# Linear-attention numerators in three rounds of 11, 11 and 10 heads instead of four rounds of 8, a memory output with one reciprocal, and a new engine order

## The chip, the core and the metric

The kernel runs on one core of a Trainium2 chip. The metric is the device time of one execution in microseconds; "span" is the length of the profiled execution, 1.7 us shorter than its timed value.

Engines are named as in the profile: PE (matmuls), PEld (their weight loads), DVE (VectorE), ACT (ScalarE), POOL (GpSimd), SP (the queue that issues most DMAs). A ratio below is the mean time of one kernel's fast runs over the mean of the kernel before's fast runs in the same rounds on the same chip. It is therefore not quite the ratio of the medians quoted beside it.

## The reference, cut to what matters

Two attention mechanisms read the same input of 2048 rows and 640 columns, with 32 heads of 20 columns; a gate mixes them.

```python
# A: linear attention with features softmax(pq), softmax(-pq)
num = einsum('bhqf,bhfd->bhqd', phi_q, kv)
den = einsum('bhqf,bhf->bhq', phi_q, z)[..., None] + 1e-06
a = (num / den).reshape(B, S, D) @ wo
# B: per segment of 512 rows, softmax attention plus a memory of earlier segments
o = sigmoid(beta) * a_mem + (1 - sigmoid(beta)) * a_dot
b = o.reshape(B, S, D) @ wo_B
return g * a + (1 - g) * b          # g = sigmoid(sum(x * gate_w))
```

## The kernel before

Every piece of work is an "op": one function that emits one or a few instructions, with what it reads and writes. Ops are numbered as they are created. A table `ORDER` gives each engine the list of op numbers it runs, in that order; each engine then runs its list in that order and waits where data are missing. A schedule model inside the kernel only turns the table into a program. Copies out of PSUM ("evacuations") can stand in the list of ACT or of DVE (a copy of the output takes 431 ns on ACT and 490 on DVE); the table decides.

```python
ORDER = {
    "PE": "29*7 73*3 77*2 80 88 104 89 82 120 90*2 ...",   # 29*7: seven ops from 29 on
    "ACT": "0 76 79 28 86 101 109 99 ...", "DVE": "27 72 81 70 83 68 93 ...",
    "POOL": "...", "SP": "1*3 10 5 11 13 4 8 7 6 9 100 ...",
}   # ... cut
```

The kernel lays out PSUM as four working banks `w` and four more that hold the attention scores `st`. The numerators of A ("a3") take four rounds for each chunk of 128 rows. One round is one bank:

```python
PARTS = (((0, 0, 7), (1, 0, 2)), ((1, 2, 5), (2, 0, 4)), ((2, 4, 4), (3, 0, 5)),
         ((3, 5, 2), (4, 0, 7)))
for qt in (2 * hf, 2 * hf + 1):          # a quarter: 8 heads, two signs, 22 columns each
    # PE: four small matmuls w <- Eq, KVD
    # ACT or DVE: dz = copy of 16 denominators out of the bank
    # DVE: xx = w * dz swapped; rr = sum over signs; rr = 1/rr; cs = w * gate * rr
    # DVE: ts = w * cs, 320 elements; then the bank is free
# POOL, once per two quarters: oA = ts[:, 0] + ts[:, 1]
```

The output of B for one group of four heads, with `Cdm` holding the gate products:

```python
for x, bk in enumerate(bks):             # local result, memory result: one bank each
    rd[x] = reciprocal(w_denominator)    # DVE, 16 elements
rd = rd * Cdm                            # DVE; a POOL op is ordered behind it (lk=True)
tdm[x] = w * rd[x]                       # DVE, 320 elements each, frees the bank
# POOL: oB = tdm[0] + tdm[1]
```

The softmax here doesn't subtract the row's maximum and nothing guards it: scores larger than these inputs give would overflow.

## Time and profile before

| | before |
|---|---|
| time, median of the first 4 runs | 291.47 us |
| span of the profile | 289.5 us |
| the 80 score exponentials (128x2048, ACT): end of the 5th, 40th, 80th | 43.7, 151.6, 268.0 us |
| late stretch (40th to 80th exponential) | 116.3 us |

The score exponentials serve as clock marks. Every kernel runs 80 of them, spread from 25 to 268 us, so the time at which the 5th, 40th and 80th ends cuts the span into a start, an early stretch (projections, key side), a late stretch (numerators, output projection) and a tail. Their ends come from the timeline, start plus duration.

The page of the kernel before, its part 1 (busy time, share of the span, instructions):

```profile
PE 280.5 (97%) x3764; PEld 191.9 (66%) x3777; DVE 229.7 (79%) x850; ACT 246.9 (85%) x353; POOL 189.2 (65%) x333
```

Part 4 of the same page, the chain of waits by engine (a queue's own time is marked with a q):

```profile
PE 80%; DVE 14%; DMA 3%; issue 1%; ACT 0%; DVEq 0%
```

PE's 97% rests on modelled ends, as the profile's own legend says. The median start-to-start distance of two matmuls of 320 columns is 136 ns where the record says 299; for 300, 340 and 512 columns the distances are 127, 144 and 215 ns, the records 291, 308 and 379. So the records of neighbours overlap. The stretches by time, here 160 to 272 us (columns: length, then busy time and instructions of PE, PEld, DVE, ACT, POOL, then granted clock, DMA share and GB/s):

```profile
160.00:272.00 112.00, 109.54 (x1607) 74.49 (x1617) 104.41 (x500) 103.60 (x123) 78.75 (x115) 1.00 0.61 133
```

DVE and ACT are both busy over 92% of this stretch (104.4 and 103.6 of 112 us). The groups of instructions of a numerator round (line, engine, operation, tiles, shape, count | busy us, mean ns of one | idle before):

```profile
L1044 DVE TENSOR_TENSOR ts<-w,cs 128x320 f32<-128x320 f32 x64 | 30.6, 486 | 1.4
L1040 DVE SCALAR_TENSOR_TENSOR cs<-w,gS,rr 128x16 f32<-128x16 f32 x64 | 14.2, 230 | 0.6
L1038 DVE RECIPROCAL rr<-rr 128x8 f32<-128x8 f32 x64 | 12.2, 198 | 0.7
L1032 DVE TENSOR_TENSOR xx<-w,dz 128x16 f32<-128x16 f32 x64 | 10.2, 169 | 0.8
L712 DVE CAST osb<-w 128x320 bf16<-128x320 f32 x6 | 2.9, 490 | 5.2 <-PE w L1086 5.2
```

A product of 16 elements takes 169 ns and one of 320 takes 486. That is 1.04 ns per element, which leaves an estimate of 152 of the 169 ns as the fixed part of the small one. That is the ground of the change. The last line is an output evacuation on DVE.

### The profile page before, as it was taken

What the parts mean: (1) busy time and instruction counts of PE and PEld (TensorE: products, weight loads), DVE (VectorE), ACT (ScalarE), POOL (GpSimd) and SP (SyncE); (2) the same over time, 40 slices, a digit from 0 to 9 for tenths busy, and PEclk for the clock granted to TensorE, in tenths of its full rate; (3) what the DMA queues carried; (4) which work ended last, traced back from release to release, by engine and by line L of the source; (5) the groups of instructions that cost most, each with busy time, mean ns of one, the idle gap of its engine ahead of it and who ended that gap; (6) DMA issues with size and microseconds to landing.
All of it is one profiled execution on the core that took longest, in us unless ns stands there. A gap on an engine that the chain in (4) does not pass through costs nothing.

```text
span 289.5 us, 9800 instructions
## 1 busy us (share of the span) xinstructions
PE 280.5 (97%) x3764; PEld 191.9 (66%) x3777; DVE 229.7 (79%) x850; ACT 246.9 (85%) x353; POOL 189.2 (65%) x333
## 2 busy tenths in 40 slices
PE   7899999999999999999999999999999999999995
PEld 3666676676676667676766566567766657667873
DVE  0774577888789999689968999988998999999820
ACT  3366799998999999999899999998999999988222
POOL 7045369789965899778282858474866586688600
PEclk9999999999999999999999999999999999999999
DMA  7998796745915432615059484824695748565342
GB/s 210 300 230 148 133 242 75 139 115 99 126 39 137 128 104 73 104 55 133 2 129 296 92 186 125 163 82 111 168 174 115 138 106 199 125 100 131 105 106 64
DMA packets 87976, 38.42 MB, mean 133 GB/s; under 512 B 69882, under 2 KB 83834, under 8 KB 87930
## 3 DMA queue, kind: packets, MB, share of 16 engines
q1 hardware_dynamic: 87274, 37.39, 57.7%
q8 instruction: 29, 0.48, 0.7%
q10 hardware_dynamic: 656, 0.41, 0.5%
q14 instruction: 17, 0.14, 0.2%
HBM read 5.61 MB, written 15.60 MB: 73 GB/s over the span
## 4 chain that ended last, share of the span: by engine, by line
PE 80%; DVE 14%; DMA 3%; issue 1%; ACT 0%; DVEq 0%
PE w L745 36%; PE w L1086 14%; PE w L1166 9%; PE st L1138 7%; PE w L988 4%; DVE ts L1044 4%; PE w L1019 3%; PE w L888 2%; DVE cs L1040 2%; DVE rr L1038 1%; PE w L1231 1%; DMA WkB<-in_B_wk_dram 1%; DVE tdm L1214 1%; DMA x_nat<-in_A_x_dram 1%; PE w L1185 1%
## 5 line engine op out<-in xcount | busy, mean ns | idle before, releaser
L1144 ACT ACTIVATE PT<-st 128x2048 bf16<-128x2048 f32 x80 | 151.4, 1893 | 4.9 <-PE st L1138 3.8
L1150 POOL TENSOR_SCALAR_AFFINE_SELECT PT<-PT 128x512 bf16<-128x512 bf16 x128 | 79.4, 637 | 41.3 <-ACT PT L1144 12.6
L745 PEld LDWEIGHTS <-xT 128*128 128x128 bf16 x800 | 72.4, 97 | 34.0 <-issue 9.1
L867 POOL TENSOR_TENSOR EkN<-Ek,krec 128x640 bf16<-128x640 bf16 x32 | 40.5, 1275 | 4.3 <-DVE phik L778 1.2
L1166 PEld LDWEIGHTS <-PT 128*128 128x128 bf16 x1280 | 39.8, 96 | 5.3 <-issue 0.8
L1166 PE MATMUL w<-vB,PT 128*128 128x21 bf16 x1280 | 41.5, 172 | 0.1
L745 PE MATMUL w<-WqB,xT 128*128 128x320 bf16 x160 | 36.0, 299 | 0.3 <-ACT kq L710 0.2
L745 PE MATMUL w<-WvA,xT 128*128 128x340 bf16 (+1 forms) x160 | 35.2, 299 | 0.0
L745 PE MATMUL w<-WkB,xT 128*128 128x320 bf16 x160 | 34.5, 299 | 0.2 <-ACT xT L691 0.2
L1048 POOL TENSOR_TENSOR oA<-ts 128x320 bf16<-128x320 f32 x32 | 27.4, 864 | 10.8 <-DVE dz L712 3.0
L745 PE MATMUL w<-WkA,xT 128*128 128x320 bf16 x160 | 33.5, 299 | 0.0
L745 PE MATMUL w<-WvB,xT 128*128 128x321 bf16 (+1 forms) x160 | 33.3, 300 | 0.1
L1086 PE MATMUL w<-WoA,oTA 128*128 128x320 bf16 x160 | 32.3, 299 | 0.2
L1086 PE MATMUL w<-WoB,oTB 128*128 128x320 bf16 x160 | 32.3, 299 | 0.0
L1138 PE MATMUL st<-kqT 32*128 32x384 bf16 (+3 forms) x512 | 31.7, 300 | 0.5 <-ACT PT L1144 0.5
L1044 DVE TENSOR_TENSOR ts<-w,cs 128x320 f32<-128x320 f32 x64 | 30.6, 486 | 1.4
L988 PE MATMUL w<-xT,WqA 128*128 128x512 bf16 x87 | 26.7, 379 | 0.8 <-DVE ts L1044 0.2
L1019 PE MATMUL w<-KVD,Eq 128*128 128x88 bf16 (+3 forms) x256 | 26.8, 207 | 0.6
L859 DVE TENSOR_REDUCE ksum<-Ek 128x32 f32<-128x640 bf16 x32 | 25.2, 804 | 2.5 <-ACT Ek L852 2.4
L1220 POOL TENSOR_TENSOR oB<-tdm 128x320 bf16<-128x320 f32 x24 | 20.6, 863 | 7.6 <-DVE dz L712 2.7
L1019 PEld LDWEIGHTS <-Eq 128*128 128x128 bf16 x256 | 19.2, 97 | 9.2 <-issue 2.8
L852 ACT ACTIVATE Ek<-w 128x320 bf16<-128x320 f32 x64 | 24.2, 452 | 1.3 <-PE w L745 1.0
(113 smaller groups left out, 445.7 us busy)
## 6 DMA issues: line engine op xcount, KB each, us to landing
kd<-kq SPq DMA_DIRECT2D x32, 256.0 KB, 2.3
od<-oA SPq DMA_DIRECT2D x16, 160.0 KB, 1.9
out_dram<-osb SPq DMA_DIRECT2D x32, 80.0 KB, 1.8
od<-oB SPq DMA_DIRECT2D x12, 160.0 KB, 1.9
WqB<-in_B_wq_dram SPq DMA_DIRECT2D x2, 400.0 KB, 4.7
WvB<-in_B_wv_dram SPq DMA_DIRECT2D x2, 400.0 KB, 4.6
WvA<-in_A_wqkv_dram SPq DMA_DIRECT2D x1, 800.0 KB, 6.3
WoA<-in_A_wo_dram SPq DMA_DIRECT2D x1, 800.0 KB, 5.3
```

The costliest lines, as they stand in the source:

```text
L745: nc.tensor.matmul(w[:, 0:width], lhsT=T["xT"][:, c, sc * P:(sc + 1) * P], rhs=T[Wn][:, c, lo:lo + width], start=(c == 0), stop=(c == KC - 1))
L859: op("DVE", 0.74, lambda sgn=sgn: nc.vector.tensor_reduce(out=T["ksum"][js][:, H * sgn:H * sgn + H], in_=T["Ek"][ik][:, sgn].rearrange("p ...
L867: op("POOL", 1.22, lambda sgn=sgn: nc.gpsimd.tensor_tensor(out=T["EkN"][ie][:, 0:2 * D].rearrange("p (h x f) -> p h x f", x=2, f=DH)[:, :, ...
L988: nc.tensor.matmul(w, lhsT=T["WqA"][:, c, t * P:(t + 1) * P], rhs=T["xT"][:, c, s * L:(s + 1) * L], start=(c == 0), stop=(c == KC - 1))
L1019: nc.tensor.matmul(w[:, c0:c0 + m * E2], lhsT=T["Eq"][j][:, sgn, qc * P:(qc + 1) * P], rhs=T["KVD"][:, sgn, OFF[t] + a:OFF[t] + a + m, :]. ...
L1044: op("DVE", dve_t(320), lambda w, c3=c3, qt=qt: nc.vector.tensor_tensor(out=T["ts"][d][:, :, 8 * (qt % 2):8 * (qt % 2) + 8], in0=vw(w)[:, ...
L1048: op("POOL", 0.82, lambda: nc.gpsimd.tensor_tensor(out=T["oA"][o][:, 320 * hf:320 * hf + 320].rearrange("p (h d) -> p h d", d=DH), in0=T[" ...
L1086: nc.tensor.matmul(w[:, 0:320], lhsT=T[nm][j][:, k5, :], rhs=T[Wo][:, k5, hf * 320:hf * 320 + 320], start=(i == 0), stop=(i == 9))
L1138: nc.tensor.matmul(st4[:, i, o:o + w], lhsT=T["kqT"][j][r:r + 32, 0, c * P:(c + 1) * P], rhs=T["kqT"][j][r:r + 32, 1, c * P:L], start=True ...
L1144: op("ACT", act_t(2048), lambda: nc.scalar.activation(out=T["PT"][slot], in_=st4, func=ACT.Exp, scale=SCALE_B), r=("st4",), w=(("PT", slot ...
L1150: nc.gpsimd.affine_select(out=v, in_=v, pattern=[[0, 4], [1, P]], compare_op=ALU.is_ge, fill=0.0, base=0, channel_multiplier=-1)
L1166: nc.tensor.matmul(w[:, j * 84 + i * V1:j * 84 + (i + 1) * V1], lhsT=T["PT"][slot][:, i, o + (j - c) * P:o + (j - c + 1) * P], rhs=T["vB"] ...
```

## The change

Its intent is to pay the fixed part less often. Eleven heads with two signs and 22 columns are 484 columns and still fit a working bank, which the kernel lays out as 512 fp32 columns, so three rounds do what four did. The memory output multiplies first and takes one reciprocal for both banks instead of two; the gate coefficients are stored inverted for it. All engine orders are new. The tile `ts` now has three buffers of one round each instead of two of a pair of rounds. The diff, cut to its core:

```diff
 ORDER = {                                   # all five lists new; SP begins
-    "SP": "1*3 10 5 11 13 4 8 7 6 9 100 132 ...",
+    "SP": "1*4 10 5 8 13 11 7 6 9 116 148 ...",
 ...
-    PARTS = (((0, 0, 7), (1, 0, 2)), ((1, 2, 5), (2, 0, 4)), ((2, 4, 4), (3, 0, 5)),
-             ((3, 5, 2), (4, 0, 7)))
+    PARTS = (((0, 0, 7), (1, 0, 5)), ((1, 5, 2), (2, 0, 8), (3, 0, 3)), ((3, 3, 4), (4, 0, 7)))
+    NHG = 11
 ...
-        for qt in (2 * hf, 2 * hf + 1):
+        for q in (2,) if hf else (0, 1):
 ...                                         # the six small ops now on 22 / 11 / 440 elements (third round: 20 / 10 / 400)
-        op("POOL", 0.82, ... oA[320 columns] = ts[:, 0] + ts[:, 1])   # once per two rounds
+            op("POOL", ..., ... oA[DH * nh columns] = ts[:, 0] + ts[:, 1])   # every round
 ...
         for x, bk in enumerate(bks):
-            rd[x] = reciprocal(w_denominator)
-        rd = rd * Cdm                        # lk=True
+            rd[x] = w_denominator * Cdm[x]
+        rd = reciprocal(rd)
 ...                                         # gates(), beta(): one more reciprocal each
```

## The prediction

> **What bounds the kernel now.** No single engine: three run nearly full. The page's first part shows PE 97%, ACT 85%, DVE 79%, POOL 65% of a 289.5 us span. PE's 97% is modelled ends. From start-to-start distances in the trace (N=320: 136 ns, N=21: 25 ns) the matmuls need about 263 us, so PE has some 16 us of holes after its first projection at 8.7 us. Busy time by stretch: between 60 and 160 us ACT is busy 95.5 of 100 us and DVE 83.8; between 160 and 272 us (the linear-attention numerators, "a3") DVE is 104.4 of 112, ACT 103.6. The chain of waits gives PE 80% and DVE 14%; its DVE pieces (ts, cs, rr, tdm) lie almost all in 160-272 us. From 272 us on it is PE alone: 80 output matmuls back to back in 11.0 us.
>
> **What the change does.**
> 1. a3 handles 11/11/10 heads per PSUM bank instead of four times 8: 48 rounds of six small operations instead of 64. The groups show 168+169+164+198+230+486 ns per round, but DVE overlaps neighbours: median start-to-start 119+117+119+120+150+408 = 1033 ns, 66 us in all. For 22/11/440 elements, at the trace's 1.04 ns per element (reciprocal about 6), I estimate 1200 ns, 58 us in all. DVE thus gains about 8.5 us of occupancy, all in 160-272 us. [...] a copy of 16 elements takes 168 ns, one of 320 takes 490.
> 2. PE: 256 numerator matmuls become 224 with the same columns: about 0.3 us.
> 3. POOL: 32 adds of 864 ns become 48 of about 570-620 ns (estimate): +1.5 us.
> 4. Memory-attention output: two reciprocals (239 ns) and one product (210) become two products (about 169) and one reciprocal of 32 (353, from the ksum reciprocal of that size): about zero. The product no longer orders a POOL instruction behind it (5.7 us of POOL waits), but POOL has slack.
> 5. New engine order. Counting the table: ACT keeps its load in sum (about -1 us), but takes about 4 us more evacuations before its tenth big exponential and 4 us fewer after its fortieth. Matmul work ahead of each score group is nearly unchanged; about 20 us remain after the last one in both.
>
> **On the critical path.** PE's work stays, so only its holes can shrink: some 16 us, perhaps 8 of them in 160-272 us. ACT, 92-95% busy, becomes the next limit there. The first 160 us and the PE-bound tail give nearly nothing. I expect about half of the late holes: 4 us.
>
> **Prediction.** 287.5 us, range 284.5 to 290.3 (8 in 10). Faster by over 2%: 0.2; within 2%: 0.77; slower by over 2%: 0.03.
>
> **What would show it.** DVE busy about 8 us (6-10) lower, nearly all in 160-272 us; ts at about 608 ns x48; DVE's share of the chain from 14% to under 9%, PE's up; ACT and POOL busy within 2 us; the last score exponential ending 3-5 us earlier than 268 us; the time from there to the end unchanged (about 21 us); 0 to 160 us within 1 us.
>
> **What would make it wrong.** The new order may close (or open) holes in the first 160 us too; DVE may have been the late phase's sole limit, then up to 8 us; or bigger rounds hold PSUM banks longer.

One clause of item 1 is cut where the mark stands, since it did not come from a run of this case; the two measured copies behind it, 168 and 490 ns, stay. Half of some 8 us of late holes is 4 us, and 291.5 less 4 is the 287.5 us forecast.

## The result, and the profile after

The changed kernel takes 289.76 us (median of 11 runs, 288.87 to 290.14) against 291.63 (16 runs): ratio 0.9932, 95% interval 0.9920 to 0.9944. That is 2.0 us, half of the 4.0 us forecast. It lies inside the range and within 2%, the likeliest of its three cases; the size of the gain is what was wrong. Part 1 of its page, busy time by engine:

```profile
PE 280.2 (97%) x3733; PEld 191.7 (67%) x3745; DVE 223.0 (78%) x766; ACT 247.7 (86%) x346; POOL 191.8 (67%) x349
```

Part 4 of its page, the chain of waits by engine:

```profile
PE 76%; DVE 17%; ACT 3%; issue 2%; DVEq 0%; ACTq 0%
```

Its stretch from 160 to 272 us, columns as before:

```profile
160.00:272.00 112.00, 109.59 (x1578) 73.93 (x1585) 100.68 (x414) 100.44 (x114) 81.73 (x130) 1.00 0.59 137
```

DVE has 84 instructions fewer over the whole span, but only 3.7 us less busy time in the window from 160 to 272 us, and its share of the chain rose. The groups that answer to those shown before:

```profile
L1046 DVE TENSOR_TENSOR ts<-w,cs 128x440 f32<-128x440 f32 x32 | 19.3, 612 | 1.4
L1046 DVE TENSOR_TENSOR ts<-w,cs 128x400 f32<-128x400 f32 x16 | 9.2, 573 | 0.8
L1042 DVE SCALAR_TENSOR_TENSOR cs<-w,gS,rr 128x22 f32<-128x22 f32 x32 | 7.4, 238 | 0.5
L1040 DVE RECIPROCAL rr<-rr 128x11 f32<-128x11 f32 x32 | 6.8, 218 | 0.5
L1034 DVE TENSOR_TENSOR xx<-w,dz 128x22 f32<-128x22 f32 x32 | 5.5, 176 | 0.3
L709 DVE CAST osb<-w 128x320 bf16<-128x320 f32 x11 | 5.2, 484 | 10.0 <-issue 5.0 <-PE w L1088 3.1 <-ACT osb L707 1.7
```

The duration of ts is what the prediction put it at (about 608 ns; 612 at 440 elements, and 573 at 400, which the prediction did not list apart). The durations also fit the 1.04 ns per element of the profile before: counted on from its 486 ns at 320 elements, it gives estimates of 569 and 611 ns for 400 and 440. The last line shows a leak: the new order puts 11 output evacuations on DVE instead of 6.

Where did 2 us come from? The marks of both kernels, from the timeline of ACT. Each fence has the 5th, the 40th and the last score exponential (columns: start us, duration us, engine, line, operation; a bracket gives the idle time before it and what ended it). Before:

```profile
41.69 1.98 ACT L1144 ACTIVATE PT<-st 128x2048 bf16<-128x2048 f32 x1
149.77 1.88 ACT L1144 ACTIVATE PT<-st 128x2048 bf16<-128x2048 f32 x1
266.10 1.88 ACT L1144 ACTIVATE PT<-st 128x2048 bf16<-128x2048 f32 x1
```

After:

```profile
40.17 1.98 ACT L1146 ACTIVATE PT<-st 128x2048 bf16<-128x2048 f32 x1
148.01 1.88 ACT L1146 ACTIVATE PT<-st 128x2048 bf16<-128x2048 f32 x1 [0.19 <-PE st L1140]
263.91 1.88 ACT L1146 ACTIVATE PT<-st 128x2048 bf16<-128x2048 f32 x1
```

The 5th ends 1.5 us earlier, at 42.2 us, some 116 us before the first numerator. The last ends 2.2 us earlier. So three quarters of the gain were made where no numerator runs. Part of that is chance: the start varies from profile to profile. Eight profiles with the old start (the kernel before and seven experiments below that leave it alone) put the 5th end at 43.7 to 44.6 us, mean 44.1. Three with the new start put it at 41.9 to 42.6, mean 42.2. The start is worth about 1.9 us. From the 5th end on, the stretches hardly vary between profiles (the early one is 108.0 or 108.1 us in all eight with the old start):

| stretch, us | before | after |
|---|---|---|
| start, to the end of the 5th exponential (means of 8 and of 3 profiles) | 44.1 | 42.2 |
| early, 5th to 40th | 108.0 | 107.7 |
| late, 40th to 80th | 116.3 | 115.9 |
| tail, from the 80th to the end | 21.5 | 21.7 |

The late stretch, for which the change was made, gave 0.4 us. (The rows add up to 2.4 us where the timed runs give 2.0; the rest lies within the spread of the start.)

### The profile page after: what moved, and what is told of

It reads as the page before. It is cut to its first block, busy times and chain, and to the rows that moved or that the text cites. A ratio compares the mean times of both kernels' runs of the same rounds, so it can differ in the third digit from the quotient of the medians.

```text
span 287.5 us, 9664 instructions
## 1 busy us (share of the span) xinstructions
PE 280.2 (97%) x3733; PEld 191.7 (67%) x3745; DVE 223.0 (78%) x766; ACT 247.7 (86%) x346; POOL 191.8 (67%) x349
## 4 chain that ended last, share of the span: by engine, by line
PE 76%; DVE 17%; ACT 3%; issue 2%; DVEq 0%; ACTq 0%
PE w L742 38%; PE w L1088 9%; PE w L1168 8%; PE st L1140 7%; DVE ts L1046 5%; PE w L987 3%; PE w L887 2%; ACT PT L1146 2%; PE w L1020 2%; DVE cs L1042 2%; DVE tdm L1215 1%; DVE rr L1040 1%; PE st L585 1%; PE w L1232 1%; DVE rr L1037 1%
## 5 line engine op out<-in xcount | busy, mean ns | idle before, releaser
L1168 PEld LDWEIGHTS <-PT 128*128 128x128 bf16 x1280 | 40.7, 96 | 5.9 <-issue 2.1
L1168 PE MATMUL w<-vB,PT 128*128 128x21 bf16 x1280 | 43.1, 172 | 0.0
L742 PE MATMUL w<-WvB,xT 128*128 128x320 bf16 (+1 forms) x160 | 37.0, 300 | 0.0
L742 PE MATMUL w<-WkB,xT 128*128 128x320 bf16 x160 | 36.6, 299 | 0.1
L1050 POOL TENSOR_TENSOR oA<-ts 128x220 bf16<-128x220 f32 (+1 forms) x48 | 30.3, 638 | 9.4 <-DVE ts L1046 4.8
L742 PE MATMUL w<-WvA,xT 128*128 128x340 bf16 (+1 forms) x160 | 33.4, 299 | 0.1
L1088 PE MATMUL w<-WoA,oTA 128*128 128x320 bf16 x160 | 31.4, 298 | 0.4 <-DVE ts L1046 0.2
L1046 DVE TENSOR_TENSOR ts<-w,cs 128x440 f32<-128x440 f32 (+1 forms) x48 | 28.4, 599 | 2.2
L1020 PE MATMUL w<-KVD,Eq 128*128 128x154 bf16 (+5 forms) x224 | 24.9, 213 | 0.3 <-DVE tdm L1215 0.2
L1215 DVE TENSOR_TENSOR tdm<-w,rd 128x320 f32<-128x320 f32 x48 | 21.6, 485 | 0.9
```

The costliest lines, as they stand in the source:

```text
L742: nc.tensor.matmul(w[:, 0:width], lhsT=T["xT"][:, c, sc * P:(sc + 1) * P], rhs=T[Wn][:, c, lo:lo + width], start=(c == 0), stop=(c == KC - 1))
L1020: nc.tensor.matmul(w[:, c0:c0 + m * E2], lhsT=T["Eq"][j][:, sgn, qc * P:(qc + 1) * P], rhs=T["KVD"][:, sgn, OFF[t] + a:OFF[t] + a + m, :]. ...
L1046: op("DVE", dve_t(2 * nh * DH), lambda w, nh=nh, vw=vw, tv=tv: nc.vector.tensor_tensor(out=tv("ts"), in0=vw(w)[:, :, :, 0:DH], in1=tv("cs" ...
L1050: op("POOL", 0.04 + 0.00244 * nh * DH, lambda h0=h0, nh=nh, tv=tv: nc.gpsimd.tensor_tensor(out=T["oA"][o][:, DH * h0:DH * (h0 + nh)].rearr ...
L1088: nc.tensor.matmul(w[:, 0:320], lhsT=T[nm][j][:, k5, :], rhs=T[Wo][:, k5, hf * 320:hf * 320 + 320], start=(i == 0), stop=(i == 9))
L1168: nc.tensor.matmul(w[:, j * 84 + i * V1:j * 84 + (i + 1) * V1], lhsT=T["PT"][slot][:, i, o + (j - c) * P:o + (j - c + 1) * P], rhs=T["vB"] ...
```

## The experiments

Theory A: the gain is the start, which the new order improved by the way, and the numerator rework gives about nothing. Rival B: the start differs by chance, and the rework gives the gain.

What differs at the start is visible in the timelines. Before, SP issues three of the four first input chunks and only four loads later the fourth; PE then waits for it, and DVE's list is headed by a small product that waits for another load. Kernel before (PE at line 681 transposes an input chunk; the bracket gives the idle time and what ended it):

```profile
0.81 1.34 SPq L537 DMA_DIRECT2D x_nat<-in_A_x_dram  x3
4.64 0.34 SPq L537 DMA_DIRECT2D x_nat<-in_A_x_dram  x1
7.21 0.30 DVE L667 TENSOR_TENSOR WphiD<-Wc,m 128x140 bf16<-128x140 bf16 x1 [6.00 <-DMA Wc<-in_A_w_phi_dram]
7.43 0.48 DVE L693 COPY xT<-w 128x640 bf16<-128x640 bf16 x1
8.22 0.45 PE L681 MATMUL w<-ident_b,x_nat 128*128 128x128 bf16 x5 [1.42 <-DMA x_nat<-in_A_x_dram]
```

Changed kernel, the same pieces: four loads in a row, DVE begins with a copy of transposed input, and PE's last transpose comes 1.8 us earlier.

```profile
0.81 1.82 SPq L534 DMA_DIRECT2D x_nat<-in_A_x_dram  x4
5.00 0.49 DVE L690 COPY xT<-w 128x640 bf16<-128x640 bf16 x1 [3.80 <-PE w L678]
6.43 0.44 PE L678 MATMUL w<-ident_b,x_nat 128*128 128x128 bf16 x5
```

### x3_early: one load earlier

```diff
-    "SP": "1*3 10 5 11 13 4 8 7 6 9 ...",
+    "SP": "1*4 10 5 11 13 8 7 6 9 ...",
```

> The kernel before, with one entry of the sync engine's order moved: the load of the fourth input chunk is issued straight behind the first three (it stood four loads later, issued at 4.64 us, and PE waited 1.42 us for it). Theory A (the whole gain of the change is this start, the numerator rework gives about nothing): ratio 0.993 to 0.996, the 1.7 us of PE holes that a DMA ends in the first 12 us gone, and every score exponential 1.3 to 1.8 us earlier. Theory B (the start differs by chance from run to run; the rework gives the gain): ratio 0.998 to 1.002.

Measured: 291.62 us against 291.50, ratio 1.0012 (0.9991 to 1.0032). No gain: this is the range that was set down for theory B. The profile shows why theory A need not fall with it. The load came early, but the phi weights' load behind it was issued at 3.54 us instead of 3.06, and DVE's list still began with the product that needs those and now started at 7.66 us instead of 7.21:

```profile
7.66 0.31 DVE L673 TENSOR_TENSOR WphiD<-Wc,m 128x140 bf16<-128x140 bf16 x1 [6.46 <-DMA Wc<-in_A_w_phi_dram]
7.88 0.49 DVE L699 COPY xT<-w 128x640 bf16<-128x640 bf16 x1
8.42 0.85 PE L751 MATMUL w<-WkB,xT 128*128 128x320 bf16 x5 [0.38 <-DVE xT L699]
```

The wait named in the profile had a second one right behind it (PE stands 0.38 us for DVE's copy). Theory A named one cause of the start too few.

### after_x3_late: the same load put back in the changed kernel

```diff
-    "SP": "1*4 10 5 8 13 11 7 6 9 ...",
+    "SP": "1*3 10 5 8 13 4 11 7 6 9 ...",
```

> The changed kernel with that one load put back to its old place in the queue. Theory A: ratio to before 0.997 to 1.002, the gain gone. Theory B: ratio 0.992 to 0.995 as the changed kernel itself.

Measured: 291.77 us, ratio 1.0027 (0.9998 to 1.0056). The whole gain is gone, as theory A said. The entry is thus needed for the gain of the given order, though x3_early shows that it does not bring the gain alone. In its profile the 5th exponential ends 2.6 us later than in the changed kernel's (44.8) and the span is 2.6 us longer; from the 5th end on both need 245.3 us. In this pair a shift of the start passes through to the end one to one.

### start_fix: both waits taken out of the kernel before

```diff
-    "SP": "1*3 10 5 11 13 4 8 7 6 9 ...",   "DVE": "27 72 81 70 83 68 93 ...",
+    "SP": "1*4 10 5 11 13 8 7 6 9 ...",     "DVE": "27 81 83 72 70 68 93 ...",
```

> The kernel before with the fourth input chunk's load issued right behind the first three, and with DVE's first six operations reordered so that the two copies of transposed input stand ahead of the three small products that wait for the phi weights' load (in x3_early DVE stood 6.5 us at their head). Numerators and the rest as before. Theory A (the changed kernel's gain is its start, and a shift of the start goes through to the end one to one, as after_x3_late showed: 2.6 us later at the fifth score exponential, 2.6 us later at the end): fifth exponential 1.0 to 1.6 us earlier, ratio 0.994 to 0.997. Theory B (the start is worth nothing without the new numerators): 0.998 to 1.002.

Measured: 290.85 us against 291.64, ratio 0.9964 (0.9952 to 0.9977): 1.0 us faster with the numerators untouched. The 5th exponential ends at 43.4 us, 0.7 under the mean of the old start (0.2 under the first profile; 1.0 to 1.6 were expected), and from there to the end it needs 245.8 us as before. PE's unbroken projections begin at 7.48 us there, at 8.51 before and at 6.71 in the changed kernel, so about half of the start's gain is accounted for. The rest of it lies in other entries of the new lists and is not taken apart.

### memout_only and after_old_memout: the memory output by itself

The first puts the new memory output, gates and beta into the kernel before; the second puts the old ones into the changed kernel. The op numbers do not change, so each keeps its kernel's order.

```diff
 # memout_only, in the kernel before
-            rd[x] = reciprocal(w_denominator)
-        rd = rd * Cdm
+            rd[x] = w_denominator * Cdm[x]
+        rd = reciprocal(rd)
```

> The kernel before with only the memory-output part of the change (product before reciprocal, coefficients inverted in gates and beta), old order, old numerators. Both theories: ratio 0.997 to 1.003; DVE busy within 1 us. A gain over 0.4% would say that the freed POOL ordering or the earlier start of the chain matters after all.

> The changed kernel with the old memory output, gates and beta, in the new order. If the new memory output is as slow by itself as memout_only showed (0.7%) the ratio to before is 0.985 to 0.990; if that loss was only the misfit to the old order, 0.992 to 0.998 (as the changed kernel or a little worse).

Measured: memout_only 293.34 us, ratio 1.0071 (1.0053 to 1.0089), slower. after_old_memout 294.93 us, ratio 1.0112 (1.0095 to 1.0128), that is 1.8% above the changed kernel. Both expectations were missed. DVE's busy time agrees with "about zero" (103.9 instead of 104.4 us between 160 and 272 us), yet either version is 2 to 5 us slow in the order that was made for the other. The first loses its time in the late stretch (118.0 us instead of 116.3), the second in the early one (112.6 instead of 107.7). What the memory output is worth cannot be read from these runs; that an order fits one set of durations and dependences can.

### thirds_old_order: the numerators by themselves

The kernel before with only the numerators in thirds. The thirds take the places of quarters 0, 2 and 3 in the old lists (in the last chunk of a segment 0, 1 and 3), and every evacuation stays on its old engine.

```diff
-    # quarter 0, quarter 1, quarter 2, quarter 3     in every engine's list
+    # third 0,   -,         third 1,   third 2
```

> The kernel before with only the numerators in thirds, laid into the old order: thirds take the places of quarters 0, 2 and 3 (the last row chunk of a segment: 0, 1 and 3), all evacuations stay on their old engines. Theory A (DVE relief does not reach the time): ratio 0.997 to 1.003 although DVE busy falls 6 to 9 us. Theory B: ratio 0.985 to 0.994, since here no evacuation moves to DVE and the whole relief is left in the late stretch.

Measured: 294.21 us, ratio 1.0099 (1.0081 to 1.0116), slower. DVE's busy time between 160 and 272 us fell from 104.4 to 98.6 us, as expected, and the late stretch grew from 116.3 to 118.7 us. Neither theory had foreseen a loss. The busy times of its window:

```profile
160.00:272.00 112.00, 107.54 (x1529) 71.18 (x1528) 98.63 (x397) 104.20 (x121) 80.12 (x128) 1.00 0.60 133
```

It says again that an order is fitted closely; it does not say what the rework is worth in an order of its own.

### before_no_rec and after_no_rec: DVE relief without a new order

To relieve an engine and leave order and dependences alone, an operation is simply not emitted. The results are wrong.

```diff
-            small(lambda w, c3=c3: nc.vector.reciprocal(out=T["rr"][c3], in_=T["rr"][c3]),
+            small(lambda w, c3=c3: None,
```

> The kernel before without the reciprocal of rr (64 DVE operations of 198 ns gone; wrong result on purpose), order unchanged. It takes about as much off DVE as the prediction counted on, without a new order and without longer rounds. If DVE is what the late stretch waits for: ratio 0.972 to 0.988. If DVE relief is not on the way (theory A): above 0.993.

> The same taken from the changed kernel (48 operations of about 217 ns; wrong result on purpose). If its late stretch still waits for the DVE chain of a numerator round: ratio to before 0.965 to 0.983, that is 1 to 3% under the changed kernel; if PE and ACT alone set the late pace there: 0.988 to 0.994.

Measured: before_no_rec 291.86 us, ratio 1.0005 (0.9992 to 1.0019). 64 DVE operations less, and the time does not move. The busy times of its late window:

```profile
160.00:272.00 112.00, 109.73 (x1615) 74.28 (x1616) 98.63 (x435) 104.25 (x125) 79.20 (x115) 1.00 0.65 138
```

Its chain of waits by engine, from its page:

```profile
PE 76%; ACT 8%; DMA 5%; DVE 4%; POOL 3%; issue 2%; SPq 0%; DVEq 0%; ACTq 0%
```

DVE is down by 5.8 us of busy time and from 14% to 4% of the chain, and ACT and POOL have come up in its place (0 to 8%, 0 to 3%). The late stretch is 116.3 us as before. A share of the chain is thus not what a faster engine would save. (The expectation of before_no_eq below speaks of about 10 us taken off DVE; in this window it is 5.8 us of busy time.)

after_no_rec took 287.50 us, ratio 0.9854 (0.9839 to 0.9869), 0.8% under the changed kernel; its late stretch is 114.3 us instead of 115.9. The ratio lies between the two ranges set down. The busy times of its window:

```profile
160.00:272.00 112.00, 110.64 (x1606) 74.78 (x1605) 95.87 (x371) 100.67 (x115) 82.00 (x130) 1.00 0.57 139
```

In the new order DVE's rounds still hold something up, in the old order they did not alone. The cut shortens each round's chain of operations as well as DVE's load, and the run does not tell which of the two counts.

### before_no_eq, before_pq4: relief of ACT alone and of PE alone

In before_no_eq the product that read the missing values reads its own first input in their place.

```diff
 # before_no_eq: query-feature exponentials of the last two segments not emitted
-            op("ACT", ..., lambda: nc.scalar.activation(out=T["eq"][e], ...
+            op("ACT", ..., lambda: None if s > 1 else nc.scalar.activation(out=T["eq"][e], ...
 # before_pq4: four of five contraction steps
-                nc.tensor.matmul(w, lhsT=T["WqA"][:, c, ...], ..., stop=(c == KC - 1))
+                if c < KC - 1:
+                    nc.tensor.matmul(w, lhsT=T["WqA"][:, c, ...], ..., stop=(c == KC - 2))
```

> The kernel before without the query-feature exponentials of the last two segments (16 ACT operations of 653 ns, 10.4 us, all after about 155 us; wrong result on purpose), order unchanged. before_no_rec took about 10 us off DVE there and the time did not move. If ACT sets the late pace: ratio 0.970 to 0.990. If it is PE's work in its fixed order: above 0.994.

> The kernel before with four of the five contraction steps of the query projection of the linear attention (20 PE operations of 215 ns gone, 4.3 us of PE, nearly all after 155 us; wrong result on purpose), order unchanged. If PE's work sets the late pace one to one: 287 us, ratio 0.984 to 0.988. If ACT does: above 0.994. In between: they share it.

Measured: before_no_eq 291.78 us, ratio 0.9998 (0.9965 to 1.0031). before_pq4 291.35 us, ratio 0.9986 (0.9958 to 1.0014). (Both still pass the comparison with the reference, as the values cut are small.) Neither moves the time. The late window of before_no_eq shows that the cut took effect on ACT (103.60 to 99.08 us):

```profile
160.00:272.00 112.00, 110.15 (x1615) 74.40 (x1614) 104.33 (x498) 99.08 (x112) 79.18 (x115) 1.00 0.63 137
```

### before_no_rec_eq, before_all_three: the cuts together

```diff
 # before_no_rec_eq: the cuts of before_no_rec and before_no_eq
-            ... lambda w, c3=c3: nc.vector.reciprocal(out=T["rr"][c3], in_=T["rr"][c3]),
+            ... lambda w, c3=c3: None,
-            ... lambda: nc.scalar.activation(out=T["eq"][e], ...
+            ... lambda: None if s > 1 else nc.scalar.activation(out=T["eq"][e], ...
 # before_all_three: these two and the cut of before_pq4
+                if c < KC - 1:
```

> The kernel before with the cuts of before_no_rec (DVE) and before_no_eq (ACT) together; results not to be right. Balanced limits (DVE, ACT and PE each alone hide the others' relief): PE's work is left, so ratio 0.990 to 0.998. If the pair DVE and ACT were the late limit: below 0.985. If something else: 0.998 to 1.002.

> The cuts on DVE, ACT and PE (before_pq4) together. Balanced limits: the time now falls by about the smallest of the three cuts, 3 to 5 us, ratio 0.983 to 0.990. If POOL, DMA or the waits built into the order set the pace: above 0.995.

Measured: both cuts on DVE and ACT 290.52 us, ratio 0.9963 (0.9941 to 0.9986); all three 290.05 us, ratio 0.9941 (0.9921 to 0.9961). The late stretch is 115.5 and 114.7 us instead of 116.3. The chain of before_all_three by engine:

```profile
PE 73%; ACT 14%; DMA 6%; DVE 4%; issue 2%; SPq 0%; ACTq 0%; DVEq 0%
```

So in the old order relief counted only when several engines got it (alone the ratios were 1.0005, 0.9998 and 0.9986), which is the sign that was set down for balanced limits. But even all three cuts together, some 4 us of PE, 5 of DVE and 5 of ACT in the late stretch, give 1.7 us and not the expected 3 to 5. The rest is held by something else, by what is left of the engines' work or by the order itself; these runs do not tell which.

### before_search, after_search and a second pair: order and structure apart

To compare quarters with thirds fairly, each needs an order fitted to it. A local search moved ops within an engine's list and evacuations between ACT and DVE, and kept what shortened the time in the kernel's own schedule model; both kernels got the same effort. The start of start_fix was put in by hand. The second pair was searched on from the first with twice the effort.

```diff
 ORDER = {
-    # the given lists
+    # the lists found by the search; no other line differs
```

> The operations of the kernel before, in a new order from a local search (moves of operations within an engine and of evacuations between ACT and DVE, judged by the schedule model inside the kernel), with the start of start_fix. If order is what counts: as fast as the changed kernel or faster, ratio 0.985 to 0.993. If the old numerators are the limit: 0.994 to 0.998, the gain of start_fix alone.

> The operations of the changed kernel in an order from the same search with the same effort. If the rework helps once the order fits: 0.5 to 1% under before_search, ratio 0.977 to 0.988. If the rework is worth nothing: equal to before_search within 0.3%.

> Old numerators, an order searched on from before_search with twice the effort. If the 0.6% between the first pair is the worth of the rework: ratio to before 0.985 to 0.990, and 0.4 to 0.9% above after_search2. If it was luck of the search: the pair within 0.3%.

> New numerators, an order searched on from after_search with twice the effort. If the rework is worth 0.6% in a fitted order: ratio to before 0.979 to 0.984. The fastest version tried, if the schedule model is right about it.

| kernel | median us | ratio to before | 5th ends | early | late |
|---|---|---|---|---|---|
| before_search (quarters) | 288.33 | 0.9884 (0.9866 to 0.9902) | 42.7 | 107.8 | 114.5 |
| after_search (thirds) | 286.50 | 0.9826 (0.9807 to 0.9845) | 43.1 | 106.4 | 113.3 |
| before_search2 (quarters) | 289.48 | 0.9944 (0.9928 to 0.9959) | 44.4 | 107.8 | 114.7 |
| after_search2 (thirds) | 286.44 | 0.9833 (0.9814 to 0.9852) | 43.5 | 106.9 | 113.0 |

The old operations in the first searched order (288.33) are faster than the changed kernel (289.76). The second search, with more effort, made them slower again (289.48, ratio 0.9944 where 0.985 to 0.990 was expected), so the schedule model judges an order only roughly. The other three expectations for ratios to the kernel before were met. The changed operations in a better order (286.50 and 286.44) beat both given kernels by 1.1% and 1.7%. Within a pair the changed operations win by 0.6% and by 1.1%, but the two ratios of the quarters differ by 0.6% between themselves. In the profiles that last difference is all in the start: from the 5th mark to the end the quarters take 243.9 and 244.1 us, the thirds 241.5 and 241.3. The start of before_search2 in the table is partly chance, since its profiled run (290.19 us) was the slowest of its six. In the late stretch the rework, numerators and memory output together, is worth 1.2 and 1.7 us, with an order fitted to each. Order alone shortens the late stretch of the changed operations from 115.9 to 113.3 us, and that of the old ones from 116.3 to 114.5. The early stretch differs by 1.4 and 0.9 us as well, where the only change is the memory output and the order; two searches do not tell those apart.

## Why the prediction was wrong

**What bounds the kernel: right in the words, not used.** "No single engine: three run nearly full" is what the runs show: cuts on DVE, ACT and PE alone gave 0.05, -0.02 and -0.14%. But the sum then treated DVE's relief as if it could close holes by itself.

**The step that failed: "I expect about half of the late holes: 4 us."** The late stretch gave 0.4 us (116.3 to 115.9). before_no_rec took 5.8 us off DVE in the old order, and it gave nothing: DVE's share of the chain fell to 4%, and ACT, DMA and POOL took its place. Most of the 2.0 us that were measured came from the start, where the prediction expected nothing, so it is luck that the time fell into its range. The prediction counted half of PE's late holes as closed by a faster DVE. It named ACT, 92% busy, as the next limit and took nothing off for it. ACT is not all of it either: with both relieved (before_no_rec_eq) the late stretch fell by only 0.8 us. The second part of the cause is the order. The same changed operations in a searched order have a late stretch of 113.3 us instead of 115.9, so the order that came with the change kept back most of what was to be had late.

The prediction also warned that bigger rounds may hold PSUM banks longer. They do: from a round's first numerator matmul to the end of its ts a bank is held for 3.2 us on average instead of 2.7. But there are fewer rounds, and the sum falls from 171 to 153 us.

**DVE "gains about 8.5 us of occupancy": half that was left.** The late window's busy time fell by 3.7 us (104.4 to 100.7). The durations of single operations were right. (Both copies that the prediction compares for the fixed part read a PSUM bank, `w`.) Two leaks were not seen. First, the estimate used medians of start-to-start distances, and those come mostly from rounds that ran in pairs, the operations of two rounds in turn. In the new order fewer operations pair up: of the operations dz, xx and rr on DVE, 164 of 248 were still running when the next one started before, 91 of 189 after. That is the order and not the thirds: in after_search it is 125 of 189. A pair before (one operation every 0.1 us, of two rounds in turn):

```profile
231.00 0.17 DVE L1032 TENSOR_TENSOR xx<-w,dz 128x16 f32<-128x16 f32 x1
231.11 0.17 DVE L712 COPY dz<-w 128x16 f32<-128x16 f32 x1
231.21 0.17 DVE L1035 TENSOR_REDUCE rr<-xx 128x8 f32<-128x16 f32 x1
231.32 0.17 DVE L1032 TENSOR_TENSOR xx<-w,dz 128x16 f32<-128x16 f32 x1
231.41 0.20 DVE L1038 RECIPROCAL rr<-rr 128x8 f32<-128x8 f32 x1
```

The start of a third that ran alone after (one operation every 0.21 us, each starting 0.03 to 0.04 us after the end of the one whose result it reads):

```profile
234.44 0.17 DVE L709 COPY dz<-w 128x20 f32<-128x20 f32 x1
234.65 0.18 DVE L1034 TENSOR_TENSOR xx<-w,dz 128x20 f32<-128x20 f32 x1
234.86 0.17 DVE L1037 TENSOR_REDUCE rr<-xx 128x10 f32<-128x20 f32 x1
235.07 0.22 DVE L1040 RECIPROCAL rr<-rr 128x10 f32<-128x10 f32 x1
```

Summing the start-to-start distances of these operations on DVE gives 75.7 us before and 69.6 after; without the few that hold more than 0.15 us of idle time it is 72.8 and 67.0. So the rework freed about 6 us. Second, the new order moved evacuations onto DVE: between 160 and 272 us four more of the output and two more of kq, against three fewer of vB. These three more of 320 columns cost about 1.2 us (3 times some 0.41 us start to start). About 1 us of the shortfall is not traced. The prediction had counted that ACT loses 4 us after its fortieth exponential and had not asked which engine takes them.

**"The first 160 us and the PE-bound tail give nearly nothing"; "0 to 160 us within 1 us": wrong for the start.** It gave 1.9 us by the means of the profiles. The wait was in the profile before (1.42 us of PE at 8.22 us), and the cure was in the diff (SP's list begins 1*4 instead of 1*3). The prediction compared the lists for load and not for what comes first. after_x3_late shows that the gain of the given order is gone without this one entry; x3_early and start_fix show that DVE's first entries count as well.

**PE: 0.3 us saved, POOL +1.5 us.** No run isolates PE's part; the 0.3 us was the estimate. Counts times median start-to-start distances of the numerator matmuls give 11.8 us before and 11.5 after. POOL's adds rose by 2.9 us (27.4 to 30.3 us, 638 ns each where 570 to 620 were estimated). That this did no harm is likely, as POOL does not appear in the chain after, but no run tests it.

**The memory output "about zero":** right for DVE's occupancy, not settled for the time, since both isolated versions suffered from an unfitting order.

**Signs named beforehand.** ts at about 608 ns: seen (612). DVE busy 6 to 10 us lower: 6.7 in sum, but over half of it in the first 60 us, where evacuations went to ACT (DVE busy 36.8 to 32.8 us between 8 and 60 us), so not for the stated reason. DVE's chain share under 9%, PE's up: DVE's rose to 17%, PE's fell from 80 to 76%. ACT and POOL busy within 2 us: ACT +0.8, POOL +2.6 us. The last exponential 3 to 5 us earlier: 2.2, mostly the start. The tail unchanged: seen (21.5 and 21.7 us).

**What stays open.** Half of the start's gain is not taken apart. What sets the late pace once three engines are relieved is not found. The worth of the memory output by itself is not known. The worth of the rework, 1.2 to 1.7 us late, rests on two pairs of one search method, the second continued from the first.

## What to carry to other kernels

In this kernel, with DVE busy 104.4 and ACT 103.6 of 112 us, a share of the chain of waits was not a saving: a cut of 5.8 us on DVE, which had 14% of the chain, or of 4.5 us on ACT moved the time by 0.05% and -0.02%, both together by -0.37%. Before counting on the relief of one engine, drop an operation there, results be wrong, and see whether the time moves. Such a cut speaks for the given order only: before_no_rec gave nothing, yet the rework gave 1.2 to 1.7 us in fitted orders. Count the distance from start to start and not the durations: small DVE operations of 0.17 to 0.20 us started every 0.10 to 0.12 us where two rounds ran in turn and every 0.21 us in a lone round, and after a copy of 320 elements lasting 490 ns the next operation started at a median of 408 ns. When a change brings a new static order, judge the order apart from the operations: compare what each queue does first, and count on which engine every movable piece of work lands in the stretch that matters. Test a new structure only in an order fitted to it, since here either half of the change, put into the other half's order, lost up to 1.8%. Order and placement of evacuations alone were worth 1.2% and 0.6% for the old operations, the repaired start included, and 1.1% and 1.0% for the new (ratios 0.9884 and 0.9944 to 1; 0.9826 and 0.9833 to 0.9932).
